# Gated delta rule and a softplus layer on one core: inverses by chunk and by pair, 64x64 tiles, word transposes, longer query runs, a new order

## The chip, the cores and the metric

The kernel runs on one core of a Trainium2 chip. The engines of the core work side by side, each through its own list of instructions in order: TensorE (PE: matmuls, and PEld: its weight loads), VectorE (DVE), ScalarE (ACT), GpSimd (POOL) and SyncE (SP, which here only issues DMAs). The metric is the device time of one execution in microseconds (us). Three runs of the kernel before took 305.52, 309.42 and 303.7 us; the median is 305.52.

## The reference

Four batches of eight heads carry a 48x48 state through 768 steps; the gated readouts of all heads, side by side, go through a layer with softplus.

```python
B, H, S, D = q.shape                      # 4, 8, 768, 48
k_n = k / (np.linalg.norm(k, axis=-1, keepdims=True) + 1e-06)
state = np.zeros((B, H, D, D))
for t in range(S):
    readout = np.einsum('bhd,bhde->bhe', q[:, :, t], state)
    y[:, :, t] = g[:, :, t] * readout
    v_old = np.einsum('bhde,bhd->bhe', state, kt)
    state = state + bt[:, :, :, None] * np.einsum('bhd,bhe->bhde', kt, vt - v_old)
...
x = y.transpose(0, 2, 1, 3).reshape(B * S, H * D)     # 3072 x 384
h = x @ w_in                                          # 384 x 2048
out = (np.maximum(h, 0) + np.log1p(np.exp(-np.abs(h)))) @ w_out
```

## The kernel before

The 768 steps are cut into 12 chunks of 64. Within a chunk the recurrence is solved at once: with the keys' inner products as a strictly lower triangular matrix and beta on the diagonal, the updates of a chunk follow from a 64x64 triangular inverse per batch and head. A partition half (64 rows) holds one pair of batches, so that a tile has 128 partitions and 16 sequences of 48 in its free dimension.

**Front of a chunk** (`front`): keys and queries are loaded from DRAM (`load`, SP's queue; one DMA brings 64 partitions x 16 sequences x 48 numbers as runs of 192 bytes), cast to 16 bits (`cast`), transposed on PE (`trs`, L289), copied out (`kev`), and multiplied with each other (`gram`, L396 and L397; `gramk` and `gramq` for the first two chunks, L326, L327 and L359). The key products go into `kk` (`kkc`), those of keys and queries are masked into `mt` (`mask`, L414).

**Norms** (`norms`): squares on ACT, sums on DVE (`red`, L445), a square root on ACT for the first two pairs, and a power on POOL afterwards (`pow`, L461). The inverse norms go into beta (`lbeta`, from L473) and into the values (`vs`, L657).

**Inverse of a pair of chunks** (`inverse`): one DVE transpose moves the key products so that each partition holds its own 32x32 block (`ln`, L481). Then the two 16x16 diagonal blocks of every 32 are inverted by forward substitution in 15 steps of a product and a sum (`step`, L504 and L511), on DVE for the first pair and on POOL for the other five. A cast (`c16`) and three DVE transposes bring the blocks back (`tn`, L524; `t32`, L534, two). PE extends 16 to 32 (`xmm`, L555; `tmm`, L576 and L582) and prepares the step from 32 to 64 (`zmm`, L608 and L611) on tiles of 32x32.

**Chain of a chunk** (`chain`): `ks` and `qs` (L649) read the state, `w` (L681) subtracts from the values, `umm` (L690 and L694), `u1`, `zu` (L715) and `u2` apply the inverse, `smm` (L735) and `s` give the next state, `ymm` (L765), `y` (L780), `ytr` (L797) and `xt` the gated readout, turned for the layer. Each product comes in two halves of 16 matmuls; umm, zmm and tmm also multiply by an identity to carry a block along.

**Layer** (`dense`): `g1` (L825) multiplies by w_in, `soft` (L837) applies softplus on ACT, `g2` (L852) multiplies by w_out, `o` and `store` bring 128 rows out. Only the chain is serial from chunk to chunk; the layer of earlier chunks fills PE beside it.

Every such step is an item with a number. The long table `_ORDER` at the end of the kernel lists all items in the order in which they are issued, with the letter of the engine (P, D, A, G for POOL, S); `Program.emit` walks through it and hands out buffers from rings as items need them. So the order within every engine is written out by hand, and an engine that waits holds up all items behind it in its own list. The eight loads of the weights (L253) are items on POOL.

Of the kernel before, what the change touches and what calls it, by code (L numbers as in the profile page):

```python
# [10 lines left out]
F32 = mybir.dt.float32  # L11
F16 = mybir.dt.float16
AF = mybir.ActivationFunctionType
# [3 lines left out]
class Ring:  # L17


    def __init__(self, tiles, name):  # L20
        self.tiles = tiles
        self.name = name
        self.free = list(range(len(tiles)))

# [13 lines left out]
class Program:  # L38
# [16 lines left out]
    def emit(self, table):  # L55
        done = set()
        for word in table.split():
            en, no = word[0], int(word[1:])
            it = self.items[no]
            assert en in it.engs and no not in done and all(d.no in done for d in it.deps)  # L60
            for b in it.bufs:
                if b.ap is None:
                    b.slot = b.ring.free.pop(0)
                    b.ap = b.ring.tiles[b.slot]
            it.fn(en)
# [5 lines left out]
        assert len(done) == len(self.items)  # L71


@with_exitstack
def kernel(
# [18 lines left out]
    U = 4 * H  # L94
    DM = H * D
    FF = moe_w_in.shape[1]
    NF = FF // P

# [13 lines left out]
    QUAD = [slice(32 * i, 32 * i + 32) for i in range(4)]  # L112

# [6 lines left out]
    beta_l = pool.tile([P, NC // 2, HC], F32, name="beta_l")  # L120
# [3 lines left out]
    r_k = ring("kf", 4, [P, 2, H, D], F32)  # L124
    r_q = ring("qf", 2, [P, 2, H, D], F32)
    r_v = ring("vf", 4, [P, 2, H, D], F32)
    r_g = ring("gf", 3, [P, 2, H, D], F32)
    r_kn = ring("kn", 5, [P, 2, H, 64], F16)
    r_qn = ring("qn", 2, [P, 2, H, 64], F16)
    r_ksq = ring("ksq", 1, [P, 2, H, D], F32)  # L130
    r_nv = ring("nv", 3, [P, 32], F32)
    r_nl = ring("nl", 2, [P, 32], F32)
    r_bl = ring("bl", 3, [P, 32], F32)
    r_kk = ring("kk", 3, [P, 2, U, HC], F16)
    r_kqt = ring("kqt", 10, [P, 2 * NP * 2 * C + HC], F16)
    r_mt = ring("mt", 10, [P, H, C], F16)
    r_ln = ring("ln", 2, [P, HC, HC], F16)
# [3 lines left out]
    r_t16 = ring("tw", 2, [P, 2, 16, 48], F16)  # L141
    r_tn = ring("tn", 2, [P, U, 16], F16)
    r_xs = ring("xs", 2, [P, U, 16], F16)
    r_td = ring("td", 3, [P, U, HC], F16)
    r_z = ring("z", 4, [P, 16, 2 * HC], F16)
    r_w = ring("w16", 4, [P, H, D], F16)
    r_u = ring("u16", 6, [P, H, D], F16)
    r_s = ring("s16", 6, [P, H, D], F16)
    r_yg = ring("yg", 2, [P, 2, H, D], F16)
    r_xt = ring("xt", 2, [P, 3, 512], F16)  # L150
    r_ga = ring("ga", 18, [P, 512], F16)
# [4 lines left out]

    nc.vector.memset(half_c, 0.5)
    nc.scalar.activation(dummy, half_c[:, :1], AF.Sqrt)
    make_identity(nc, ident32)
    nc.vector.tensor_copy(ident, ident32)  # L160
    for t in r_kn.tiles + r_qn.tiles:
        nc.vector.memset(t[:, :, :, D:], 0.0)
    for r in range(2):
        for hf in range(2):
            l0 = 32 * (2 * r + hf)
            src = beta[2 * r : 2 * r + 2].rearrange(
                "p h (c l r) -> (p h) l c r", l=2, r=64
            )
            for cl in range(2):
                nc.gpsimd.dma_start(  # L170
                    out=beta_l[l0 + 16 * cl : l0 + 16 * cl + 16],
                    in_=src[:, cl, :, 32 * hf : 32 * hf + 32],
                )
# [11 lines left out]
    for t in r_t16.tiles:  # L185
        nc.vector.memset(t, 0.0)
    for t in r_kqt.tiles:
        nc.vector.memset(t[:, 4 * NP * C :], 0.0)
    pat = pool.tile([P, HC], F16, name="pat")
    nc.vector.tensor_tensor(pat, ident[:, :HC], ident[:, 64 : 64 + HC], ALU.add)  # L190
    for t in r_z.tiles:
        nc.vector.tensor_copy(t[:, :, :HC], pat[:, None, :].broadcast_to([P, 16, HC]))
# [19 lines left out]


    tiles, last = {}, {}

    def load(name, x, r, c, b2):
# [5 lines left out]
        def fn(en):  # L222
            ENG[en].dma_start(
                out=b.ap[64 * b2 : 64 * b2 + 64].rearrange("t p h d -> t (p h) d"),
                in_=x[2 * b2 : 2 * b2 + 2, :, t0 : t0 + C].rearrange(
                    "p h t d -> t (p h) d"
                ),
            )

        its.append(  # L230
            add("load", f"{name}{c}.{b2}", "A" if name == "k" and c < 2 and b2 else "S", fn,
                bufs=[b])
        )

    for c in range(NC):
        for name, x, r in (("k", k, r_k), ("q", q, r_q), ("v", v, r_v), ("g", g, r_g)):
# [18 lines left out]


    kn, kn_it, kqt, kqt_it, mt, mt_it = {}, {}, {}, {}, {}, {}

    def kq_of(c, p):
        return kqt[c, p].ap[:, : 4 * NP * C].rearrange("p (n t) -> p n t", n=2 * NP)  # L260

    def front(c, kk):
        cl = c % 2
        parts = 2 if c < 2 else 1
        for p in range(2):
            kqt[c, p] = Buf(r_kqt)
        its, x_of = {}, {}
        for name, ring_ in (("k", r_kn), ("q", r_qn)):
            f, fl = tiles[name, c]
            x = Buf(ring_)  # L270
            x_it = []
            for h in range(parts):
                sl = slice(h, h + 1) if parts == 2 else slice(0, 2)
                x_it.append(
                    add("cast", f"{name}n{c}.{h}", "DGA",
                        lambda en, f=f, x=x, sl=sl: copy(en, x.ap[:, sl, :, :D], f.ap[:, sl]),
                        deps=fl, bufs=[f, x], size=768 // parts)
                )
            x_of[name] = (x, x_it)
            its[name] = []  # L280
            for h in range(parts):
                tp = Buf(p_d)
                ps = [h] if parts == 2 else [0, 1]

                def trs(en, x=x, tp=tp, ps=ps):
                    o = f16ps(tp.ap).rearrange("p (a n t) -> p a n t", a=2, n=NP)
                    for p in ps:
                        for i in range(NP):
                            nc.tensor.transpose(  # L289
                                o[:, p, i],  # L290
                                x.ap[:, p, 2 * i : 2 * i + 2].rearrange("p h d -> p (h d)"),
                                ident,
                            )

                t1 = add("trs", f"{name}{c}.{h}", "P", trs,
                         deps=[x_it[h] if parts == 2 else x_it[0]], bufs=[x, tp],
                         mm=4 * len(ps), mode="full")
                for p in ps:

                    def kev(en, p=p, tp=tp, name=name):  # L300
                        s = f16ps(tp.ap).rearrange("p (a n t) -> p a n t", a=2, t=C)[:, p]
                        kq = kq_of(c, p)
                        copy(en, kq[:, :, :C] if name == "k" else kq[:, :, C:], s)

                    its[name].append(
                        add("kev", f"{name}{c}.{p}", "AD", kev, deps=[t1], bufs=[tp, kqt[c, p]])
                    )
        kn[c], kn_it[c] = x_of["k"]
        mt[c] = [Buf(r_mt), Buf(r_mt)]
        mt_it[c] = []  # L310
        kk_it = []

        def u_of(ap, p, m):
            return ap[:, :, 16 * cl + 8 * p + m : 16 * cl + 8 * p + 8 : 2]

        if c < 2:
            gk = [Buf(p_d), Buf(p_d)]
            for p in range(2):

                def gramk(en, p=p):  # L320
                    for i in range(NP):
                        for r in range(2):
                            for m in range(2):
                                x = kq_of(c, p)[FEAT[m], 2 * i + r, :C]
                                o = gk[m].ap.rearrange("p (n t) -> p n t", n=H)
                                nc.tensor.matmul(o[QUAD[2 * r], NP * p + i], x[:, :HC], x)  # L326
                                nc.tensor.matmul(  # L327
                                    o[QUAD[2 * r + 1], NP * p + i],
                                    x[:, HC:],
                                    x.rearrange("f (x t) -> f x t", x=2)[:, ::-1],  # L330
                                )

                t2 = add("gramk", f"{c}.{p}", "P", gramk, deps=[its["k"][p]],
                         bufs=gk + [kqt[c, p]], mm=32, mode="6432")
                for m in range(2):

                    def kkc2(en, p=p, m=m):
                        copy(
                            en,
                            u_of(kk.ap, p, m).rearrange("p x n t -> p n x t"),  # L340
                            gk[m].ap.rearrange("p (n x t) -> p n x t", n=H, x=2)[
                                :, NP * p : NP * p + NP
                            ],
# [645 lines left out]
```

## Time and profile before

| what | us |
|---|---|
| median of three runs | 305.52 |
| span of the profiled execution | 304.6 |
| PE busy | 241.7 |
| DVE busy | 184.7 |
| ACT busy | 131.4 |
| POOL busy | 120.5 |
| L825 and L852, the layer's matmuls | 82.0 and 77.7 |
| L504 and L511 on POOL, the substitution | 29.0 and 27.7 |
| L837, softplus | 56.3 |

The profile is one execution, seen by the hardware profiler. Its page cuts the span into 40 slices and gives the busy share of each engine in tenths (9 is 90% or more), the clock that TensorE was granted, and the share of the 16 DMA engines. A row of a group reads: line, engine, operation, what it writes and reads, shapes, count | busy time, mean duration in ns | idle time of the engine before it and what ended that. Of the timeline a row reads: start, duration, engine, line, shapes, count [idle before]. In the chain of waits a row is a piece of the path that ended last: start, duration, what. "issue" there is time in which the engine waited for nothing that the profile shows. Waits read: who waited for whom: us in total, times, longest. DMA queues read: packets, megabytes, share of the 16 engines.

### The profile page before, as it was taken

How to read it: one execution, taken by the hardware profiler on the slowest of the kernel's cores; microseconds unless marked ns; L12 is line 12 of the kernel's file. 1: busy time of each engine (PE TensorE's matmuls, PEld its weight loads, DVE VectorE, ACT ScalarE, POOL GpSimd, SP SyncE). 2: the span in 40 equal slices, each digit the busy share in tenths (PEclk: the TensorE clock that was granted, in tenths of full speed). 3: DMA queues.
4: the chain of work that ended last, by engine and by line, in shares of the span. 5: the costliest groups of instructions: out<-in, count | busy, mean ns of one | idle time of the engine just before them, and what ended most of it. 6: DMA issues, size and time to landing. Idle time of an engine off the chain costs nothing.

```text
span 304.6 us, 13469 instructions
## 1 busy us (share of the span) xinstructions
PE 241.7 (79%) x6112; PEld 160.8 (53%) x6112; DVE 184.7 (61%) x348; ACT 131.4 (43%) x250; POOL 120.5 (40%) x219
## 2 busy tenths in 40 slices
PE   1432347789959996869877999969899969999993
PEld 1232236568637763446643565635566635577771
DVE  7789936367696776974873467668486193432100
ACT  4541413347513666244423466613553425433441
POOL 7205335008892588458516203885007810000000
PEclk9999999999969999799985799995999988999999
DMA  9999999999900197983979521341035110002113
GB/s 126 152 140 151 171 143 181 185 168 142 130 2 4 31 163 130 156 132 55 167 109 146 109 56 30 62 68 30 4 83 106 27 28 18 14 22 63 26 26 78
DMA packets 107704, 27.69 MB, mean 91 GB/s; under 512 B 100864, under 2 KB 107648, under 8 KB 107648
## 3 DMA queue, kind: packets, MB, share of 16 engines
q1 hardware_dynamic: 101600, 23.21, 48.5%
q0 software_dynamic: 3968, 3.25, 6.7%
q8 instruction: 47, 0.77, 1.1%
q10 hardware_dynamic: 2080, 0.39, 0.9%
q14 instruction: 9, 0.07, 0.1%
HBM read 25.26 MB, written 4.72 MB: 98 GB/s over the span
## 4 chain that ended last, share of the span: by engine, by line
PE 46%; DVE 21%; POOL 17%; issue 10%; ACT 3%; DMA 2%; DVEq 0%; POOLq 0%; ACTq 0%
PE h L825 14%; PE o L852 14%; POOL tmp L504 8%; POOL tt L511 7%; DVE td L534 4%; DVE tn L524 3%; DVE ln L481 3%; PE d L649 3%; DMA kf<-in_k_dram 2%; PE d L715 2%; DVE tt L511 2%; PE d L289 2%; POOL nn L496 2%; DVE tmp L504 2%; PE d L765 1%
## 5 line engine op out<-in xcount | busy, mean ns | idle before, releaser
L825 PE MATMUL h<-xt,w_in 128*128 128x512 f16 (+1 forms) x384 | 82.0, 352 | 0.0
L852 PE MATMUL o<-w_out,ga 128*128 128x384 f16 x384 | 77.7, 345 | 2.3 <-issue 1.7
L837 ACT ACTIVATE ga<-h 128x512 f16<-128x512 f32 x96 | 56.3, 596 | 40.3 <-PE h L825 33.6
L852 PEld LDWEIGHTS <-ga 128*128 128x128 f16 x384 | 37.3, 102 | 28.9 <-issue 8.9
L825 PEld LDWEIGHTS <-w_in 128*128 128x128 f16 x384 | 36.5, 103 | 22.6 <-issue 5.3
L504 POOL TENSOR_TENSOR tmp<-nn,tt 128x30 f32<-128x30 f32 (+7 forms) x75 | 29.0, 387 | 5.9
L511 POOL TENSOR_TENSOR tt<-tt,tmp 128x30 f32<-128x30 f32 (+7 forms) x75 | 27.7, 369 | 5.9
L534 DVE STREAM_TRANSPOSE td<-tw 128x512 f16<-128x512 f16 x12 | 28.7, 2452 | 0.0
L461 POOL TENSOR_TENSOR nv<-nv,half_c 128x32 f32<-128x32 f32 x4 | 21.8, 5446 | 9.1 <-DVE nv L445 9.1
L200 DVE CAST u<-d 128x384 f16<-128x384 f32 x23 | 12.5, 552 | 19.4 <-PE d L715 15.3
L414 DVE TENSOR_TENSOR mt<-d,mask 128x256 f16<-128x256 f32 x40 | 16.8, 435 | 9.8 <-ACT kk L198 6.7
L198 ACT ACTIVATE u<-d 128x384 f16<-128x384 f32 x25 | 12.1, 492 | 23.4 <-PE d L715 12.7
L198 ACT ACTIVATE kqt<-d 128x512 f16<-128x512 f16 x26 | 15.1, 597 | 16.0 <-PE d L289 10.4
L555 PE MATMUL d<-tn,kk 16*32 16x16 f16 x768 | 7.3, 173 | 16.8 <-DVE tn L524 13.3
L289 PE MATMUL d<-ident,kn 128*128 128x128 f16 x96 | 9.1, 250 | 13.1 <-DVE kn L200 6.1
L198 ACT ACTIVATE osb<-o 128x384 f32<-128x384 f32 x14 | 6.9, 492 | 27.2 <-PE o L852 26.9
L496 POOL TENSOR_TENSOR nn<-ln,bl 128x256 f32<-128x256 f16 x10 | 6.3, 650 | 30.9 <-DVE ln L481 30.9
L649 PE MATMUL d<-s,kqt 48*64 48x48 f16 x704 | 16.7, 192 | 1.7 <-issue 1.4
L649 PEld LDWEIGHTS <-kqt 48*64 48x64 f16 x704 | 13.5, 112 | 8.4 <-issue 7.7
L555 PEld LDWEIGHTS <-kk 16*32 16x32 f16 x768 | 7.1, 93 | 18.8 <-issue 15.2
L657 POOL TENSOR_TENSOR vf<-vf,nv 128x768 f32<-128x768 f32 x8 | 11.8, 1472 | 13.2 <-DMA vf<-in_v_dram 13.2
L780 DVE TENSOR_TENSOR yg<-d,gf 128x384 f16<-128x384 f32 x24 | 12.8, 551 | 5.7 <-PE d L765 5.6
(100 smaller groups left out, 405.1 us busy)
## 6 DMA issues: line engine op xcount, KB each, us to landing
qf<-in_q_dram SPq DMA_DIRECT2D x24, 192.0 KB, 5.7
vf<-in_v_dram SPq DMA_DIRECT2D x24, 192.0 KB, 5.8
gf<-in_g_dram SPq DMA_DIRECT2D x24, 192.0 KB, 5.5
out_dram<-osb SPq DMA_DIRECT2D x48, 96.0 KB, 2.2
kf<-in_k_dram SPq DMA_DIRECT2D x22, 192.0 KB, 5.5
w_in<-in_moe_w_in_dram POOLq DMA_DIRECT2D x4, 384.0 KB, 6.6
w_out<-in_moe_w_out_dram POOLq DMA_DIRECT2D x4, 384.0 KB, 10.2
kf<-in_k_dram ACTq DMA_DIRECT2D x2, 192.0 KB, 4.5
```

The lines of the kernel that those rows point to most:

```text
L198: nc.scalar.activation(o, x, AF.Copy, scale=float(sign))
L289: nc.tensor.transpose(o[:, p, i], x.ap[:, p, 2 * i : 2 * i + 2].rearrange("p h d -> p (h d)"), ident,)
L414: nc.vector.tensor_tensor(mt[c][m].ap[:, NP * p : NP * p + NP], gb[m].ap.rearrange("p (n b) -> p n b", n=NP)[:, :, C:], mask[:, None, :].b ...
L461: lambda en: nc.gpsimd.tensor_tensor(nv.ap, nv.ap, half_c, ALU.pow),
L504: eng.tensor_tensor(t, nn.ap[:, :, j + 1 :, j : j + 1].broadcast_to([P, 2, n, w]), tt.ap[:, :, j : j + 1, :w].broadcast_to([P, 2, n, w]), ...
L511: eng.tensor_tensor(rows, rows, t, ALU.add)
L534: nc.vector.transpose(td.ap.rearrange("p u i -> p i u")[:, 16 * b : 16 * b + 16], tw.ap[:, b, :, c0 : c0 + 32],)
L555: nc.tensor.matmul(uv(xp.ap)[QUAD[qd], u], kk.ap[r, 0, u, :], tn.ap[r, u, :])
L649: nc.tensor.matmul(hd(o.ap)[HALF[r], NP * p + i], kq_of(c, p)[FEAT[m], 2 * i + r, off : off + C], s0[r].ap[FEAT[m], NP * p + i], **start(p ...
L825: nc.tensor.matmul(hp.ap[:, n * b : n * b + n], w_in[:, j, f * P : (f + 1) * P], xt.ap[:, j, t0 : t0 + n], start=(j == 0), stop=(j == 2),)
L837: lambda en, hp=hp, o=gb: nc.scalar.activation(o.ap, hp.ap, AF.Softplus),
L852: nc.tensor.matmul(op.ap[:, :DM], b.ap[:, col + c0 : col + c0 + 128], w_out[:, f, :], start=(f == 0), stop=(f == NF - 1),)
```

## The change

The kernel computes the same. What changes:

- Inversions: the chunks are grouped as [0], [1], [2, 3], ... [10, 11]. Chunk 0 is inverted on DVE, the other six groups on POOL. Chunk 0's work no longer waits for chunk 1's keys in the data; the order decides what runs first.
- The key products, the inverse and the identities beside them lie in 64-wide tiles (`kk`, `td` of 96 columns, `z`, `xs`, with fixed identity columns that are filled once), so that all small products run on 64x64 tiles, 32 matmuls to an item, without separate identity matmuls. In most of them successive matmuls go through all four tiles (`CROSS`).
- The transposes of the inverse move 32-bit words, pairs of 16-bit numbers. For a pair `ln` moves 1024 words, and each of the three transposes out 512; `pick`, and masks in `ca` and `cb`, sort the two chunks of a pair.
- From chunk 1 on, keys are scaled by the inverse norm before the transpose (`kmul`, in place of the cast), so beta and values stay as they are.
- Queries are loaded as runs of 1536 bytes (8 steps x 48 numbers) and put into place by the copy behind the transpose (`qev`).
- Squares, keys, queries, values and gates share one ring of 12 buffers.
- Constants: the first buffer of each ring is set up on DVE, the others by POOL as items (`gset`).
- A new order, with the weights' loads first on POOL.

```diff
+GROUPS = [[0], [1], [2, 3], [4, 5], [6, 7], [8, 9], [10, 11]]
+INV_ENG = "DGGGGGG"
...
+    r_f = ring("f", 12, [P, 2, H, D], F32)
...
+    CROSS = [
+        (r, p, i, m)
+        for i in range(NP)
+        for m in range(2)
+        for p in range(2)
+        for r in range(2)
+    ]
...
+            if name == "q":
+                src = x[:, b2::2, t0 : t0 + C].rearrange(
+                    "b i (g j) d -> b i g (j d)", j=8
+                )
+                ENG[en].dma_start(out=b.ap[:, b2].rearrange("p h d -> p (h d)"), in_=src)
+                return
...
+                def kmul(en, sl=sl, nv=nv):
+                    n = 2 if parts == 1 else 1
+                    ENG[en].tensor_tensor(
+                        kn[c].ap[:, sl, :, :D], kf.ap[:, sl],
+                        nv.ap[:, :NU].rearrange("p (a h) -> p a h", a=2)[:, sl, :, None]
+                        .broadcast_to([P, n, H, D]),
+                        ALU.mult,
+                    )
...
+        def lanes_out(dst, src, blocks, step_):
+            i = words(src.rearrange("p s x j -> p (s x j)")).rearrange(
+                "p (s x w) -> p x w s", s=HC, x=2)
+            o = words(dst.rearrange("p c u t -> p (c u t)"))
+            if pair:
+                o = o.rearrange("p (n k w) -> p k w n", n=32, w=8)[:, blocks::step_]
+                nc.vector.transpose(o, i)
...
+            def xmm(en, cl=cl, xp=xp):
+                for u in range(NU):
+                    for r in range(2):
+                        nc.tensor.matmul(
+                            uv(xp.ap)[HALF[r], u],
+                            kk.ap[HALF[r], cl, u, HC:],
+                            dn.ap[HALF[r], cl, u],
+                        )
...
+        def umm(en):
+            for r, p, i, m in CROSS:
+                nc.tensor.matmul(
+                    hd(up[r].ap)[HALF[r ^ p], 2 * i + m],
+                    td.ap[HALF[r], cl, H * p + 2 * i + m, :C],
+                    w1[m].ap[HALF[r], NP * p + i],
+                )
```

The order's beginning, for POOL, was: casts of keys and queries, the scaling of v0, weights from the ninth item on. It is now: weights w1.3, w1.0, w1.2, w0.2, w0.1, w0.0, the diagonal of chunk 1, w0.3, the first setup, w1.1, the second setup, the scaling of v0, a copy of it, and then chunk 1's inverse. DVE's beginning has chunk 0's keys, the sum of chunk 1's squares, chunk 0's transpose and steps, with the scaling of chunk 1's keys and a mask after the eighth step. PE's list has the X product of chunk 1 behind the second g1 of chunk 0, and that of chunks 4 and 5 right behind the chain of chunk 3.

More of the change, by code (lines that the diff above doesn't have):

```diff
@@ L194 @@
+    setup = [None]
+    for n in range(1, 4):
+        setup.append(add("gset", f"{n}", "G", lambda en, n=n: later(en, n)))
+    for r_ in (r_kn, r_qn, r_tw, r_ta, r_kk, r_td, r_z, r_xs):
+        for n in range(1, len(r_.tiles)):
+            r_.init[n] = setup[n]
     ENG = {"D": nc.vector, "A": nc.scalar, "G": nc.gpsimd, "S": nc.sync}
```

1094 lines of the change are left out of this document (547 added, 547 removed).

## The prediction

> **What bounds the kernel now.** I read the page first: the 40 slices, then the chain that ended last.
>
> ```profile
> PE   1432347789959996869877999969899969999993
> DVE  7789936367696776974873467668486193432100
> PEclk9999999999969999799985799995999988999999
> DMA  9999999999900197983979521341035110002113
> ...
> PE 46%; DVE 21%; POOL 17%; issue 10%; ACT 3%; DMA 2%; DVEq 0%; POOLq 0%; ACTq 0%
> ```
>
> One slice is 7.6 us. TensorE (PE) is nearly idle for seven slices while the DMA is full; afterwards it is busy, with dips that a lower clock digit accompanies. No engine is the bound throughout: PE holds 46% of the chain, inversions (DVE, POOL) most of the rest.
>
> Next the timeline of PE around the second pair's inverse, and the waits.
>
> ```profile
> 86.89 1.19 PE L555 MATMUL d<-tn,kk 16*32 16x16 f16 x128 [3.56 <-DVE tn L524]
> 88.01 5.00 PE L852 MATMUL o<-w_out,ga 128*128 128x384 f16 x16
> ...
> PE d L555 <- DVE tn L524: 13.3, 5, 3.6
> ```
>
> PE waits 3.6 us for the transposed inverse, and then 16 dense matmuls take 5.0 us. The chain of waits gives the full pace, and the pace of small products:
>
> ```profile
> 42.13 1.04 PE d L715 x31
> 43.18 2.28 issue
> 47.66 0.44 PE d L359 x28
> ...
> 171.73 0.50 PE d L715 x30
> 293.09 1.31 PE h L825 x12
> ```
>
> At full pace six 128x256 matmuls take 0.655 us, and four 128x384 ones 0.65, half of the 1.25 at 88 us. So each inversion costs its wait plus some 3 us of half-pace matmuls. The "issue" gaps of 2 us lie where no data was missing; the instruction queue's 47 packets of 16 KB suggest code arriving through full DMA queues.
>
> **PE's own work.** I priced every step in PE's order at its undisturbed duration: 96 g1 x 0.655 + 96 g2 x 0.65 = 125.3 us dense, and small steps of 76.7 (8 transposes 0.45, a gram half 0.35, xmm 0.49, tmm 0.60, zmm 0.52, each sixteen 64x64 products 0.25). Sum 202. PE needs 300.4 - 6.1 = 294.3, so 92 is excess, 42 of it before 60 us. From the X product of chunks 4 and 5 (122.5 us) to the last matmul it needs 143.8 and takes 177.9: excess 34.
>
> **Small products on 64x64 tiles.** Products fall from 6112 matmuls to 4840. Per chunk nine groups of 32 (xmm, tmm, zmm, ks, qs, umm, zu, smm, ymm) and two grams of 16 remain beside transposes. Gramq is the one step of before that rotates over four 64x64 tiles: 28 in 0.44 is 15.7 ns, against 33.5 for the two-tile zu (31 in 1.04) at the same half pace. zu at full pace is 16.7 ns (30 in 0.50), so four tiles come to 7.8, and 32 products to 0.25; I add 0.05 for changes of tile shape. The ends are 0.25 and, if rotation gains nothing, 0.53. xmm and tmm alternate between two tiles: 0.45. Per chunk: transposes 0.9 and 0.34, grams 0.6, xmm and tmm 0.9, seven groups 2.1: 4.8, and 183 in all (179 to 203).
>
> [...]
>
> **The inverse as words.** These rows are by form:
>
> ```profile
> L534 DVE STREAM_TRANSPOSE td<-tw 128x512 f16<-128x512 f16 x12 | 28.7, 2452 | 0.0
> L461 POOL TENSOR_TENSOR nv<-nv,half_c 128x32 f32<-128x32 f32 x4 | 21.8, 5446 | 9.1 <-DVE nv L445 9.1
> L524 DVE STREAM_TRANSPOSE tn<-tw 128x512 f16<-128x512 f16 x6 | 14.3, 2377 | 2.6 <-POOL tw L200 2.4
> L481 DVE STREAM_TRANSPOSE ln<-kk 128x1024 f16<-128x1024 f16 x6 | 11.4, 1907 | 2.2 <-ACT kk L198 2.0
> L473 DVE STREAM_TRANSPOSE nl<-nv 128x32 f32<-128x32 f32 x6 | 1.2, 202 | 0.1
> ```
>
> A pair still has one transpose of 1024 elements in and three of 512 out; only the element doubles. Scattered 2-byte writes cost 4.7 ns each (L534), scattered reads 1.9 (L481). Words appear only in L473, 202 ns for 32, hardly more than other DVE operations of that size. Ends: 1 ns a word (ln 1.0, out 0.6) or per element as now (1.9, 2.4). I take 1.9 and 1.0, nearer to the word row. DVE's other operations, counted in the changed program and priced by their rows, make 155.6 (48 masks x 0.435, 24 u x 0.552, 22 w x 0.556, 8 key products x 0.95, 12 xs x 0.68 the largest), so DVE totals 186 (173 to about 210) against 184.7: the values' scaling and the low transposes go; key scaling, xs and a seventh inversion come.
>
> **POOL.** Six inversions instead of five at 15 us (69.0 to 83.9), nine powers of 16 instead of four of 32: 2.7 each if halved, 5.4 if the cost is fixed; I take 2.7.
>
> **Weights and queries.** All eight weight loads move ahead of everything on POOL, issued from about 4.6 us.
>
> ```profile
> q1 hardware_dynamic: 101600, 23.21, 48.5%
> q0 software_dynamic: 3968, 3.25, 6.7%
> ```
>
> Counting packets in steps of 3 us: from 51 to 60 us queues q0 and q1 move one for one (590 against 596), q1 at 196 a us instead of 780. 3712 weight packets thus hold the input loads back from 6.6 to about 27 us; before, this happened at 31 to 39 and 46 to 61. A query load falls from 1024 packets of 21 ns to 128 of about 100 (the stores' packets of that size): 1.35 to 0.8 us, 13 us of DMA in all, and under the weights it hardly counts. SP's order then gives: k0 at 5.5 as before, k1 10, q0 13.5, v0 29, the second half of g0 39.
>
> **The front, step by step.** DVE has the reduction of k1 ahead of chunk 0's transpose, so that starts at 12.3 (13.8 before) in spite of the smaller chunk; prep and 15 steps take 11.3 as before, plus 3 for chunk 1's scaling, gram pieces and transpose placed between them, plus lockouts:
>
> ```profile
> 24.77 0.80 DVE L504 TENSOR_TENSOR tmp<-nn,tt 128x30 f32<-128x30 f32 x1
> 25.61 1.41 DVE L511 TENSOR_TENSOR tt<-tt,tmp 128x30 f32<-128x30 f32 x1
> ```
>
> These two need 0.21 elsewhere; a POOL cast (24.70, 0.83) and product (25.50, 1.48) run beside them, and each ends with it. POOL's 15 setup operations now fall among the steps: 0 to 6 us, I take 2. X starts about 31 (30.0 before); ymm at 38; y waits for g0 at 39 and DVE's order; the first g1 comes at 43 instead of 52.2.
>
> [...]
>
> POOL's scaling of v0 waits until 29, and chunk 1's inverse is queued behind it: 31 to 46.5. PE has all but two g1 queued behind chunk 1's X product (48), so the early dense work hardly starts before. Three powers, a cast, and chunk 3's gram behind that lead to prep2 at 61.5, the pair's inverse at 76.5, X at 79 (86.9 before); power and inverse again: X of chunks 4 and 5 at **99.5** instead of 122.5. Fixed-cost powers add up to 10.
>
> **Costed at nothing.** ACT comes to 142 by its rows (131.4 before; evictions of 1024 columns at twice 0.6 less a little), half of the span: hidden, except in a chain's own copies, which stay as many. On SP the store of chunk 0's second half stands ahead of the loads of v2 and g2; it waits for the output product at about 58, and v2 is wanted at 81: 20 us of cover; without it chunk 2's chain would wait as long. All loads share 12 buffers instead of 4, 2, 4 and 3; the first that waits for a slow reader is q7, for v0's (31 us), wanted by POOL before 57.
>
> **Sum.** 44.5 of PE's 183 are then done (16 g1, 16 g2, six fronts, four inversions, three and a half chains), 138.5 remain. Later inversions start 10 us or more ahead of their place in PE's order, so most of their waits (3.0 and 3.1 at 202 and 244 us among them) and the half pace behind them go: of 34 excess I keep 20, for code gaps, chain latencies and DVE, which is then busy about 120 of 155 us. The end behind the last matmul stays 4.2 (304.6 - 300.4). 99.5 + 138.5 + 20 + 4.2 = **262**. The profiled span, 304.6, is 0.9 below the median of 305.5, so the forecast stands for both.
>
> **Rivals.**
> - *Transposes cost per element as now.* DVE 210, inverses some 3 us later each: excess 34 and X at 105 give 282 (276 to 296). For it: L534 and L524 agree at 4.7. Chance 0.20.
> - *All waits go.* Excess 8, work 135: 247. Chance 0.08.
> [...]
> - *The tiles do not do what they should*: 0.53 a group, stalls stay: work left 154, X at 106, excess 34: 298 to 302. Chance 0.08.
> - *DVE becomes the bound, slower.* If scattered word writes cost by bytes, 9.3 ns, a transpose out takes 4.7 and ln 3.7: 107 us, DVE 263. In the last 44 us DVE is idle 35 whatever it costs (9.8 busy from 260 us on), and 20 of inner waits at least: 318. It decides from about 4 us per transpose. Against it: L473. Chance 0.12.
>
> The forecast itself, 250 to 276, gets 0.50. A measurement of this kernel separates about 2% from no change. Faster: 0.50 + 0.20 + 0.08 + 0.02 = 0.80; same 0.08; slower 0.12. The range reaches from half of the lighter case to the edge of no change: 243 to 300.
>
> **What would show it.** The word transposes near 1.0 us; a four-tile group of 32 in 0.3; g1 from 43; X of chunks 4 and 5 at 100; later X products without a wait; input loads at about 200 packets a us until 27. It is wrong if DVE's transposes exceed 2.4 us, or if PE's dips return at the inversions.

## The result and the profile after

The changed kernel takes 293.52 us (median of 4 runs, 292.94 to 297.3) against 306.19 for the kernel before on the same chip (4 runs, 303.7 to 309.42): ratio 0.962, interval 0.953 to 0.972. Medians, here and below, are over all runs of a kernel; ratios leave out runs that lie over 1.5% above its fastest. It is faster, as forecast, and inside the range, but by 12.7 us where 43 were forecast. The profiled execution has a span of 292.2.

The page after: five rows of the 40 slices (one is 7.3 us), the two large DMA queues (packets, megabytes, share) and the chain that ended last.

```profile
PE   0303117489995884699997899669997999999993
DVE  7999038467996768897785945268856852230000
POOL 8921688876488989961885058850486000000000
PEclk9999999959999597589999999959999999999998
DMA  7999998970499498547599371211010120121212
...
q1 hardware_dynamic: 82176, 23.60, 47.9%
q0 software_dynamic: 4096, 3.25, 6.9%
...
POOL 39%; PE 31%; DVE 10%; issue 8%; DMA 6%; ACT 4%; POOLq 0%; ACTq 0%; DVEq 0%
```

POOL now holds 39% of the chain (17% before) and is busy for most of the first 125 us, but for 15 to 29 us, where it waits behind the weights (below). PE is still nearly idle for six slices, and dips at 88 to 95 us, at 110 to 124 and at 183 to 197, with the clock at half in or behind each (95.9 to 102.7, 112.9 to 126.5 and 191.4 to 198.2). The longer query runs took 19,400 packets from q1 and hardly any of its time (48.5% before).

This table is read from the timeline of PE: when a step starts, in us. "Layer of 2, 3" is the first g1 of chunks 2 and 3; "rest" is from there to the last matmul.

| kernel | first g1 | X of chunk 3 | layer of 2, 3 | last matmul | rest |
|---|---|---|---|---|---|
| before | 52.2 | 87.4 | 112.0 | 300.4 | 188.4 |
| forecast | 43 | 79 | | 257.8 | |
| changed | 53.9 | 97.5 | 124.3 | 287.9 | 163.6 |

Read across, this is the whole result. Once the layer of chunks 2 and 3 runs, the changed kernel needs 24.8 us less than before (PE is busy for 17.6 us less there, 151.8 instead of 169.3, and idle for 7.2 less, 11.9 instead of 19.1); but that point comes 12.3 us later. The difference is the 12.5 that the last matmul moved.

### The profile page after: what moved, and what is told of

Its sections match the earlier page's. It is cut to its first block, busy times and chain, and to the rows that moved or that the text cites. A ratio compares the mean times of both kernels' runs of the same rounds, so it can differ in the third digit from the quotient of the medians.

```text
span 292.2 us, 11017 instructions
## 1 busy us (share of the span) xinstructions
PE 221.4 (76%) x4840; PEld 146.6 (50%) x4840; DVE 175.3 (60%) x351; ACT 145.8 (50%) x250; POOL 149.8 (51%) x271
## 4 chain that ended last, share of the span: by engine, by line
POOL 39%; PE 31%; DVE 10%; issue 8%; DMA 6%; ACT 4%; POOLq 0%; ACTq 0%; DVEq 0%
POOL tt L605 13%; PE o L923 12%; POOL tmp L598 11%; PE h L896 11%; DMA w_out<-in_moe_w_out_dram 6%; POOL tw L622 4%; POOL nn L588 3%; DVE ln L549 3%; DVE mt L476 2%; POOL nv L351 2%; ACT tw L620 2%; PE d L689 1%; PE d L843 1%; PE d L494 1%; PE d L669 1%
## 5 line engine op out<-in xcount | busy, mean ns | idle before, releaser
L896 PEld LDWEIGHTS <-w_in 128*128 128x128 f16 x384 | 36.2, 100 | 24.8 <-issue 4.1
L605 POOL TENSOR_TENSOR tt<-tt,tmp 128x30 f32<-128x30 f32 (+7 forms) x90 | 36.3, 403 | 7.0
L254 ACT ACTIVATE kqt<-d 128x1024 f16<-128x1024 f16 (+1 forms) x21 | 20.0, 960 | 22.5 <-PE d L400 20.6
L351 POOL TENSOR_TENSOR nv<-nv,half_c 128x16 f32<-128x16 f32 x9 | 26.2, 2914 | 4.6 <-DVE nv L357 2.8
L689 PE MATMUL d<-tb,xs 64*64 64x32 f16 x384 | 9.1, 188 | 12.8 <-DVE xs L678 11.7
L669 PE MATMUL d<-dn,kk 64*64 64x32 f16 x384 | 10.2, 198 | 9.4 <-DVE dn L651 6.0
L494 PE MATMUL d<-kqt 48*64 48x128 f16 (+1 forms) x448 | 11.9, 225 | 5.5 <-ACT kqt L254 3.8
L400 PEld LDWEIGHTS <-kn 128*128 128x128 f16 x96 | 7.7, 116 | 16.1 <-issue 7.6
L689 PEld LDWEIGHTS <-xs 64*64 64x64 f16 x384 | 8.2, 120 | 15.0 <-DVE xs L678 12.5
L254 ACT ACTIVATE kk<-d 128x256 f16<-128x256 f32 x32 | 11.6, 392 | 7.9 <-PE d L494 4.8
L669 PEld LDWEIGHTS <-kk 64*64 64x64 f16 x384 | 9.7, 134 | 11.0 <-issue 7.2
L773 DVE TENSOR_TENSOR w<-f,d 128x384 f16<-128x384 f32 x22 | 11.2, 549 | 4.9 <-PE d L742 3.6
## 6 DMA issues: line engine op xcount, KB each, us to landing
beta_l<-in_beta_dram POOLq DMA_DIRECT2D x8, 10.0 KB, 11.8
```

The source lines that it names most:

```text
L254: nc.scalar.activation(o, x, AF.Copy, scale=float(sign))
L351: lambda en: nc.gpsimd.tensor_tensor(nv.ap[:, :NU], nv.ap[:, :NU], half_c[:, :NU], ALU.pow),
L400: nc.tensor.transpose(o[:, NP * p + i], kn[c].ap[:, p, 2 * i : 2 * i + 2].rearrange("p h d -> p (h d)"), ident,)
L605: eng.tensor_tensor(rows, rows, t, ALU.add)
L669: nc.tensor.matmul(uv(xp.ap)[HALF[r], u], kk.ap[HALF[r], cl, u, HC:], dn.ap[HALF[r], cl, u],)
L689: nc.tensor.matmul(uv(ep.ap)[HALF[r], u], xs.ap[HALF[r], u], tb.ap[HALF[r], cl, u])
```

## The experiments

Times are medians; ratios are against the kernel before, run on the same chip beside each. "Layer", "rest" are those of the table above, read from each kernel's profiled run (e3's took 294.5 us, far above its median, so its steps are left out).

| run | median | ratio, interval | X of 3 | layer | rest |
|---|---|---|---|---|---|
| changed | 293.5 | 0.962 (0.953 to 0.972) | 97.5 | 124.3 | 163.6 |
| e1 beta loads on SP | 290.9 | 0.946 (0.939 to 0.953) | 90.1 | 117.7 | 163.9 |
| e2 one cast on VectorE | 294.0 | 0.956 (0.949 to 0.963) | 92.7 | 119.7 | 167.4 |
| e3 six pair copies on VectorE | 289.4 | 0.944 (0.940 to 0.948) | | | |
| e4 these three | 288.3 | 0.942 (0.938 to 0.946) | 90.1 | 117.1 | 162.1 |
| e5 e4, w_out later | 288.9 | 0.950 (0.940 to 0.960) | 91.9 | 119.4 | 162.4 |
| e6 e4, inverse 1 on VectorE | 283.9 | 0.933 (0.922 to 0.943) | 88.8 | 116.9 | 162.5 |
| e7 two tiles in turn | 298.8 | 0.983 (0.971 to 0.995) | 97.6 | 128.3 | 167.0 |
| e8 transposes twice | 313.4 | 1.030 (1.021 to 1.040) | 99.4 | 128.8 | 178.2 |
| e9 e6, new order | 281.1 | 0.920 (0.911 to 0.928) | 89.5 | 115.3 | 160.7 |
| e10 new order alone | 288.2 | 0.941 (0.934 to 0.948) | 94.3 | 120.1 | 161.6 |
| e11 e6, w_out later | 285.0 | 0.926 (0.915 to 0.938) | 89.4 | 116.6 | 162.1 |
| e12 e6, all weights later | 285.3 | 0.929 (0.920 to 0.937) | 89.9 | 116.8 | 163.1 |
| e13 inverse 1 shortened | 296.8 | 0.976 (0.971 to 0.980) | 92.1 | 121.7 | 168.9 |
| e14 inverse 2, 3 shortened | 293.5 | 0.965 (0.960 to 0.969) | 93.4 | 120.1 | 167.7 |
| e15 inverse 4, 5 shortened | 293.9 | 0.966 (0.956 to 0.977) | 96.4 | 123.8 | 163.9 |

### The front: POOL's queue behind the weights (e1 to e4)

In the changed kernel these groups stand out, by form (count | busy, mean ns | idle time before and what ended it).

```profile
L235 POOL DMA_DIRECT2D beta_l<-in_beta_dram x8 | 4.2, 530 | 14.1 <-DMA w_in<-in_moe_w_in_dram 9.4 <-DMA w_out<-in_moe_w_out_dram 4.7
L651 DVE STREAM_TRANSPOSE tb<-tw 128x256 uint32<-128x256 uint32 x2 | 1.2, 625 | 11.2 <-POOL tw L256 11.2
L256 POOL CAST tw<-tt 128x512 f16<-128x512 f32 x1 | 2.4, 2397 | 0.0
L622 POOL TENSOR_SCALAR tw<-tt,mx 128x512 f16<-128x512 f32 x3 | 10.3, 3417 | 0.2
L620 ACT ACTIVATE tw<-tt,mx 128x512 f16<-128x512 f32 x4 | 10.1, 2516 | 0.8 <-POOL tt L605 0.8
L622 DVE TENSOR_SCALAR tw<-tt,mx 128x512 f16<-128x512 f32 x3 | 4.1, 1366 | 1.9 <-POOL tt L605 1.9
```

The second setup step issues eight small beta loads on POOL, behind the eight weight loads. Seven of the eight issues wait until an earlier weight load has landed, 0.3 to 3.7 us each and 14.1 in all; value scaling, the cast of chunk 0's inverse and the inverse of chunk 1 stand behind them, and VectorE's transpose of that cast waits 11.2. The last three rows are one copy on three engines: 512 columns, each 16-bit number written 64 bytes behind the one before, take 3.4, 2.5 or 1.4 us.

e1 takes the eight loads out of the setup step:

```diff
-                        eng.dma_start(
-                            out=beta_l[l0 : l0 + 16, 2:],
...
+    add("beta", "late", "S", late_beta)
...
-S14 P173
+S14 S1181 P173
```

> The eight late beta loads are issued by SyncE (between its other loads) instead of by GpSimd behind the weight loads; nothing else changes. Theory (the lost time is POOL's queue standing behind the weights at the front): the rest of the setup step ends near 19 us instead of 36, so the cast of chunk 0's inverse (38.7 to 41.0 in the changed kernel) comes at 29 to 32; T product of chunk 0 at 33 to 35 instead of 42.6, first g1 at 45 to 47 instead of 53.9, X product of chunk 1 at 49 to 52 instead of 58.4, and the end 7 to 10 earlier: 284 to 287. Rival A (what was won at the front is given back, because PE or another queue is late later anyway): first g1 as early, but the end 0 to 3 earlier, 290 to 294. Rival B (the input loads under the weights are what holds the front): T product of chunk 0 early, but first g1 still at 52 or later, waiting for the gate rows, and the end unchanged.

e2 and e3 change letters of the order only:

```diff
-D153 D155 G154
+D153 D155 D154
```

> Only the cast of chunk 0's inverse goes from GpSimd to VectorE, behind the one of its first half. Theory: T product of chunk 0 at 32 to 34 instead of 42.6, but umm of chunk 0 still waits for the value scaling on POOL (36.1 to 38.1), so first g1 comes 6 to 7 earlier, at 47; POOL's own work loses only the 2.4 us of the cast, so chunk 1's inverse and all that is queued behind it come 2.4 earlier, and so does the end: 290 to 292. Rival (PE's front is what sets the end, not POOL's queue): the end follows the first g1, 286 to 288.

```diff
-G286 ... G367 ... G529 ... G530 ... G532 ... G611
+D286 ... D367 ... D529 ... D530 ... D532 ... D611
```

> Only the six masked copies of the pairs that POOL makes (three of 512 columns at 3.4 us, three of 256 at 1.4) go to VectorE (1.37 for 512, about 0.4 for 256). Theory: each stands either in front of a transpose or of POOL's next power and inverse, so the X product of chunk 3 comes 2 earlier (95.5 instead of 97.5), POOL's next inverse 3.4 earlier, X of chunk 4 at 116 to 118 instead of 121, X of chunk 9 4 earlier than 191.5; the end 3 to 6 earlier, 287 to 290. Rival (these copies lie beside PE's work): X products a little earlier, the end within 1 us of the changed kernel.

> The three edits of the other runs together. Theory: the gains add up in front of the inverse of chunks 4 and 5, since it is one queue of POOL: its X product at 106 to 110 instead of 121, and the end at 278 to 283. Rival A: PE is then the bound from the first g1 on, and the end comes to 286 to 290 whatever X does.

e1's T product of chunk 0 came at 36.6 (42.6), the first g1 at 49.1, X of chunk 1 at 51.7 (58.4), and the last matmul of the profiled run 6.3 earlier: the way of the theory, but of its figures only X of chunk 1 was met. The median fell only 2.6, to 290.9, into the range of rival A, with runs from 287.5 to 293.9; the clock, below, goes with that spread. e2 brought the first g1 to 45.3, 8.7 earlier, and the layer's start 4.6 earlier, but not the end, at a lower clock (0.881 to 0.926 in its runs). e3 came to 289.4, inside its range; where that gain arises is not shown. e4 gave 288.3, the value of rival A: the gains do not add up.

### What the gains are worth (e7, e8)

e7 turns the loops of the six four-tile groups:

```diff
     CROSS = [
         (r, p, i, m)
+        for p in range(2)
         for i in range(NP)
         for m in range(2)
-        for p in range(2)
         for r in range(2)
     ]
...
```

> The changed kernel, with the loops of the six groups that run over four 64x64 tiles turned so that consecutive matmuls alternate between two tiles only; the same matmuls otherwise. Theory: each group takes 0.45 to 0.5 instead of 0.25, 70 groups in all, 14 to 17 us more of PE's own work; where PE has no slack (behind the X product of chunk 4, 60% of them) it reaches the end: 9 to 12 later than the changed kernel's 293.5, 302 to 306, which would mean that most of what the change gained came from here. Rival (the groups lie in chains that wait for copies anyway): 294 to 297.

e8 issues each `nc.vector.transpose` of the inverses twice:

```diff
                 nc.vector.transpose(o, i)
+                nc.vector.transpose(o, i)
```

> The changed kernel, with every transpose of the inverses (into and out of the lanes) issued twice in a row on VectorE: 31 us more of DVE, about what they would cost at one price per 16-bit element. The prediction's rival said of that price: 20 us more (282 against 262). Theory (only the inverses in front of the X product of chunk 4 are on the path, with some 2 to 3 us each, later ones come ahead of their place): 8 to 12 later than the changed kernel's 293.5, 301 to 306, with X of chunk 3 at 100 to 103 and X of chunk 4 at 127 to 131. Rival (DVE has room everywhere): 294 to 297.

Two rows of PE and two of VectorE from the changed kernel, by form:

```profile
L800 PE MATMUL d<-u,z 64*64 64x48 f16 x384 | 6.2, 198 | 2.1 <-DVE u L256 1.7 <-ACT u L254 0.3
L843 PE MATMUL d<-u,mt 64*64 64x48 f16 x384 | 9.3, 193 | 0.6 <-issue 0.6
...
L549 DVE STREAM_TRANSPOSE ln<-kk 128x1024 uint32<-128x1024 uint32 x5 | 9.7, 1935 | 0.2
L647 DVE STREAM_TRANSPOSE td<-tw 128x512 uint32<-128x512 uint32 x5 | 5.4, 1074 | 2.3 <-POOL tw L622 2.3
```

The same row of zu (L800) in e7:

```profile
L800 PE MATMUL d<-u,z 64*64 64x48 f16 x384 | 8.1, 199 | 1.6 <-DVE u L256 0.7 <-ACT f L334 0.6 <-ACT u L254 0.2
```

32 products start within 0.25 us over four tiles (changed kernel) and within 0.38 to 0.40 over two (e7). So four tiles save 0.13 to 0.15 an item, 9 to 10 us of PE for some 70 items, and 5.3 us of time: less than the theory's 9 to 12, more than the rival allowed. ymm (L843) has as many matmuls as zu and 9.3 us instead of 6.2. Each of its products reads and writes the same partition half, so it has two tiles only, in the changed kernel too, as zu has in e7 (8.1); why it takes longer than that, no run shows.

The doubled transposes add 34 us to VectorE (209.6 busy instead of 175.3) and cost 19.9 us, the price that the prediction's rival had put on transposes at one price per element. Where it arises differs from the expectation: only 4.5 lie ahead of the layer of chunks 2 and 3, and 14.6 in the rest, where VectorE's queue holds the copies of the chains. PE is idle there for 19.7 us instead of 11.9, and its mean clock in that stretch is 0.92 instead of 0.97, so part of the 14.6 is pace and not waiting. Waits of PE in e8 that lie wholly or mostly in the rest:

```profile
PE d L679 <- DVE dn L656: 3.9, 2, 3.6
...
PE d L797 <- DVE z L256: 2.9, 1, 2.9
PE h L906 <- DVE xt L256: 2.8, 2, 2.4
```

### Place of the weights, the series on POOL, the order (e5, e6, e9 to e12)

e5, e11 and e12 move words of POOL's list behind the scaling of v0 (`G633`) and its copy (`G634`); e5 the four w_out loads (`G103` to `G106`), e11 these and the second setup step (`G1`), e12 the w_in loads too:

```diff
-G106 G103 ... G105 G101 ... G100 ... G99 ... G102 ... G104 ... G1 ... G633 ... G634
+G101 ... G100 ... G99 ... G102 ... G633 ... G634 G103 G104 G105 G106 G1
```

> The kernel with the three edits together, and besides the four w_out loads (half of the weight bytes) moved on POOL's queue from the very front to behind the scaling of v0. Theory (under the weights the input loads crawl, so POOL waits for v0 until 31.6 even when its queue is free): v0 and with it the scaling at 22 to 25, chunk 1's inverse from 28.5 (its own transpose) instead of 33.7, X product of chunk 1 at 45 to 47 instead of 51.0, of chunk 3 at 84 to 86 instead of 90.1, and the end 3 to 5 earlier than with the three edits (profiled span 283.4, median 288.3): median 283 to 285. Rival (the same bytes have to come before the gate rows and the keys of chunks 2 and 3 anyway): the scaling earlier, but first g1 not before 46 and X of chunk 3 within 1 us of 90.1, the end unchanged.

> The kernel with the three edits and chunk 1's inverse on VectorE (median 283.9), and only on POOL's queue: the four w_out loads and then the second setup step come behind the scaling of v0 and its copy. In the earlier run with late w_out loads both setup steps ran back to back on POOL from 9.0 to 15.6 and held a VectorE operation of 0.17 us for 6.06 us; here only the first one runs there. Theory (the weights in front hold back v0, the gate rows and the keys): scaling of v0 at 22 to 25 instead of 30.9, umm of chunk 0 at 34 to 36 instead of 37.1, X of chunk 3 at 86 to 88 instead of 88.8, median 281 to 283. Rival (the same bytes then hold back queries, gates and the keys of chunks 2 and 3): scaling early, X of chunk 3 at 89 or later, median 284 to 287.

> As the run beside it, but all eight weight loads behind the scaling of v0 and its copy, w_in first. Theory: without weights in front the scaling comes at 15 to 19, keys of chunks 2 and 3 and the gate rows land 5 or more earlier, umm of chunk 0 at 33 to 35, the first g1 at 45 to 48 (49.9 before), X of chunk 3 at 84 to 87, median 278 to 282. Rival (w_in is then what the first g1 waits for): first g1 at 51 or later, X of chunk 1 and the front behind it in PE's list late with it, median 285 to 290.

The scaling came at 21.4 us in e11 and 14.4 in e12 (30.9 in e6), in e5 the copy behind it at 23.7, and the layer's start did not move by more than 0.3 between e6, e11 and e12: the rivals of e11 and e12 hold. Where the weights stand is neutral in these kernels, where chunk 1's inverse does not queue behind them on POOL. With that inverse on POOL only e5 moved weights, and its front was slower for another reason, seen in VectorE's timeline (first fence) and POOL's (second):

```profile
8.89 6.06 DVE L347 TENSOR_SCALAR nv<-nv 128x16 f32<-128x16 f32 x1 [0.28 <-ACT nv L336]
14.99 0.31 DVE L349 COPY nv<-nv 128x16 f32<-128x16 f32 x1
```

```profile
9.49 1.17 POOL L214 COPY kk<-pat 128x512 f16<-128x512 f16 x2
10.60 1.16 POOL L214 COPY td<-pat 128x512 f16<-128x512 f16 x2
...
12.65 1.16 POOL L214 COPY kk<-pat 128x512 f16<-128x512 f16 x2
13.76 1.16 POOL L214 COPY td<-pat 128x512 f16<-128x512 f16 x2
14.87 0.73 POOL L214 COPY z<-pat 128x256 f16<-128x256 f16 x2
```

An operation that takes 0.17 us in the changed kernel took 6.06 here: it ended at 14.95, when POOL's row of copies had come to its last pair (from 14.87). So one operation lasted nearly as long as a whole row of instructions beside it; what it waited for, the trace does not show.

e6 adds chunk 1's inverse on VectorE, and e9 rearranges e6's lists and 136 engine letters; e10 rearranges the changed kernel's lists alone.

```diff
-INV_ENG = "DGGGGGG"
+INV_ENG = "DDGGGGG"
```

> The kernel with the three edits together, and besides the whole inverse of chunk 1 (30 small steps) on VectorE behind chunk 0's, between the copies of chunk 0's chain, instead of on POOL. Theory (the chain of inverses on POOL, four of them before the X product of chunk 4, sets the first half): POOL is free for the power of chunk 3 at 34 instead of 50.2; the pair inverse of chunks 2 and 3 starts at 60 to 64 instead of 69.8, X of chunk 3 at 80 to 85 instead of 90.1, X of chunk 4 at 104 to 108 instead of 113.8, and the end 6 to 9 earlier than the median of the three edits (288.3): 279 to 283. Rival A (keys of chunks 2 and 3 have to pass DVE and PE first, which the steps now delay): inverse of 2 and 3 not before 68, the end unchanged or later. Rival B (X products come early but PE is bound behind them): X of chunk 4 early, the end only 0 to 3 earlier.

> The kernel with the three edits and chunk 1's inverse on VectorE, with the same items in a new order: the lists of PE, VectorE, ScalarE and GpSimd rearranged, and 136 copies, casts, scalings and masked copies given to another engine that can do them; loads, weights, PE's matmuls and transposes unchanged. Theory (what is left of the forecast was lost in queues, by items that were ready and stood behind others that waited; from the X product of chunk 4 on PE has 139 us of own work and takes 166 in this kernel without the new order, 27 of excess, and 30 more between the first g1 and there): the excess falls by 12 to 18, in the second half above all; the layer's work of chunk 2 starts 5 to 8 earlier than 129, the X products of chunks 8 and 10 7 to 15 earlier than 192.3 and 215.3, and the median comes to 266 to 273, against 283.9 without the new order. Rival A (the inverses set the pace, not the queues): X of chunk 3 still at 88 to 92, PE waits there as before, the median 280 to 285. Rival B (contention of VectorE and GpSimd, which is then higher, eats it): single operations on VectorE several times their length, the median above 285.

> The changed kernel with only the order of its items rearranged: every item stays on its engine, chunk 1's inverse on POOL, the late beta loads inside the second setup (which now comes behind chunk 0's cast on POOL's queue). Theory: as in the run beside it; the front gains some 3 to 6 by the setup step alone (T product of chunk 0 at 36 to 39 instead of 42.6), the rest comes from the queues: the layer's work of chunk 2 from 126 to 130 instead of 136.2, X of chunk 8 at 186 to 190 instead of 203.6, the median 270 to 278 instead of 293.5. Rival A (engine assignments and the price of the copies on POOL, not the order, are what costs): 287 to 292. Rival B (the order is worth the 7 of the front that the first run showed, no more): 284 to 288.

e6's median is 4.4 below e4's, less than its theory's 6 to 9: POOL was free early, but the pair's inverse still started at 68.4, since chunk 3's keys passed VectorE and PE late (its rival A for the place). In the profiled runs the last matmul even comes at 279.4 against e4's 279.2, so the timeline does not show the 4.4; e4's runs had clocks of 0.907 to 0.946, e6's of 0.934 to 0.951. e9 is the fastest of all, 281.1, and beats both kernels; but it missed its 266 to 273 and came out as its rival A had it (X of chunk 3 at 89.5, 280 to 285). Its page, whose chain reaches back over its last part only:

```profile
PE   0321254989995866889999899999999999999993
...
PEclk9999999999999865686999999999999999999999
...
PE 45%; ACT 2%; DVE 1%; issue 0%; DVEq 0%; ACTq 0%
```

From 133 us to the last slice PE never falls below eight tenths, and the clock is full. Of its rest of 160.7 PE is idle for 3.9 us only, against 11.9 in the changed kernel; so, some half pace before 133 us apart, that rest is PE's own pace through this list, and less waiting can hardly lower it further. e10 stopped at 288.2, where its rival A had it: the order alone, the setup's new place in it included, gains 5.3.

### Which serial stage sets the start of the layer (e13 to e15)

Each leaves out the last seven of fifteen substitution steps of one inverse (so that inverse is incomplete):

```diff
         def step(en, j):
+            if gi == 2 and j >= 8:
+                return
             n, w = 15 - j, j + 1
```

> The changed kernel without the last seven of the fifteen substitution steps of chunk 1's inverse on POOL (6.2 us less there, so the inverse of chunk 1 is not complete). Theory (a series on POOL: setup, inverse of 1, powers, inverse of 2 and 3): X of chunk 1 at 52 instead of 58.4, the pair's inverse (77.0) and X of chunk 3 (97.5) 4 to 6 earlier, the layer's work of chunks 2 and 3 at 118 to 120 instead of 124.3, the median 287 to 289. Rival (the keys of chunk 3, through VectorE's and PE's queue, hold the pair's inverse, not POOL): the pair's inverse at most 2 earlier, the median 291 to 294.

> The changed kernel without the last seven substitution steps of the inverse of chunks 2 and 3 (6.2 us less on POOL, the inverse not complete). Theory (it is on the path to the layer's work in full): X of chunk 3 at 91 to 92 instead of 97.5, the layer's work of chunks 2 and 3 at 118 to 119, the median 287 to 288. Rival (PE still works off the layer of chunk 1 in front of that X product): X at 95 or later, the median 291 to 294.

> The changed kernel without the last seven substitution steps of the inverse of chunks 4 and 5 (some 5 us less on POOL, the inverse not complete). Theory (its masked copies wait for POOL at 116.6 on VectorE and ScalarE, with the copies of chunk 3's chain queued behind them, so it delays the layer of chunks 2 and 3, which does not need it): chain of chunk 3 ends 3 to 4 earlier, the layer's work at 120 to 121 instead of 124.3, the median 289 to 291. Rival (only chunk 3's own chain sets it): 123.5 to 124.3, the median 292.5 to 294.

All three theories fail by the median, and e13 is slower than the changed kernel although it does less. By the timeline e13 and e14 do move the layer's start, by 2.6 and 4.2 (e15 by 0.5, as its rival had it), but the rest grows by 5.3 and 4.1. Busy time by stretch in the changed kernel, with PE's clock third from the right:

```profile
220.00:225.00 5.00, 3.92 (x56) 2.20 (x55) 2.56 (x3) 3.92 (x6) 3.73 (x8) 1.00 0.02 3
225.00:230.00 5.00, 3.92 (x169) 2.89 (x169) 4.61 (x7) 2.58 (x5) 0.00 (x0) 1.00 0.18 41
```

The same in e14:

```profile
220.00:225.00 5.00, 2.80 (x109) 1.95 (x107) 4.34 (x6) 3.99 (x5) 1.31 (x1) 0.92 0.00 0
225.00:230.00 5.00, 5.00 (x105) 3.03 (x104) 2.73 (x5) 0.56 (x2) 0.00 (x0) 0.50 0.19 43
```

And the wait in between, in the changed kernel's timeline of PE and in e14's:

```profile
226.07 0.34 PE L923 MATMUL o<-w_out,ga 128*128 128x384 f16 x1 [2.16 <-ACT ga L908]
```

```profile
223.04 0.34 PE L925 MATMUL o<-w_out,ga 128*128 128x384 f16 x1 [2.20 <-ACT ga L910]
```

The same wait for softplus, 2.2 us long, is followed by the full clock in one kernel and by half of it in the other, from 224.2 to 231.0, where four of g2's matmuls take 1.46 us instead of 0.82 until 231. What decides between the two outcomes, no run shows. Between 50 us and the last matmul, windows of 0.2 us show nine stretches of half clock in the traces before and after: two of 3.4 us, two of 6.8 and one of 13.7 before, three of 6.8 and one of 13.7 in the changed kernel.

In e1's four runs the time is longer where the mean clock is lower (clock, time):

```
0.944 287.54    0.935 290.11    0.923 291.69    0.909 293.88
```

6.3 us lie between equal programs. e13's two runs of 296.7 had 0.904 and 0.907 (a third, of 333.8, had 0.696). e14's three runs (293.88, 293.54 and 292.64) had 0.920 to 0.924; the changed kernel's one run at 0.919 took 297.3, its other three, at 0.938, took 293. So the 4.2 won at the layer's start seem to be there and lost to the lower clock; with one run to compare, this is likely and not shown.

## Why the prediction was right in sign and wrong in size

**PE's own work: right in the count, short in the prices.** By the prediction's prices the work behind the X product of chunk 4 is 138.6 (forecast 138.5); the small products took longer than priced, as the third point shows.

**Word transposes: right**, 1.07 and 1.94 us (1.0 and 1.9 forecast), and POOL's power of 16, 2.91 (2.7). That their price matters, 20 us by e8, was the size given to the rival.

**Four tiles: right in mechanism, too small in the terms.** 0.25 us for 32 was measured, but "seven groups 2.1" counted ymm among them (0.60 to the next item), and four others took 0.37 with the change of shape, not 0.30: 2.7 a chunk; X and T products took 1.2 instead of 0.9. That is 0.9 a chunk, by estimate some 7 us for the eight chunks or so behind the X product of chunk 4. The bound of 0.53 for two tiles was too high (0.38 to 0.40 in e7), and the rival's other half, 'stalls stay', was nearer: without rotation the kernel takes 298.8, inside its 298 to 302, but by another sum.

**The front: the first step that failed.** "POOL's 15 setup operations now fall among the steps: 0 to 6 us, I take 2" left out that this item also issues eight DMAs on a queue full of weights: 14.1 us of waiting and 4.2 of issue. The first g1 came at 53.9 instead of 43, X of chunk 1 at 58.4 instead of 48. e1 takes back 4.8 of the one and 6.7 of the other. That the weights hold v0 back is right (its scaling came at 30.9 us in e6 and at 14.4 in e12), but the start of the layer did not move with it.

**The copies behind an inverse: a term that is too small.** "Costed at nothing" speaks of a chain's own copies, "which stay as many"; for those of the inverse the sum allows no more than the 2.5 us between its end and X of chunk 3 (76.5 to 79), and 5.0 were measured (92.5 to 97.5). Before, one cast stood behind a pair's inverse, in runs of 16 numbers (its median on VectorE 0.46 us; the mean below holds one of 1.68). Now four masked copies stand there, two of them of 512 columns with a step of 64 bytes, at 1.4 to 3.4 us each. The step is what differs most; no run changes it alone. The row before:

```profile
L200 DVE CAST tw<-tt 128x512 f16<-128x512 f32 x5 | 4.0, 799 | 7.8 <-POOL tt L511 7.8
```

The chain of waits after the pair's inverse in the changed kernel:

```profile
92.50 3.36 POOL tw L622
95.86 2.57 POOL nv L351
98.43 1.17 POOL nn L588 x2
...
112.39 2.88 POOL nv L351
...
116.56 0.46 ACT tw L620
118.60 0.69 ACT ta L620
119.29 0.38 ACT u L254
```

A copy and a power stand before the next inverse, another power inside it, and ACT's copies of that inverse in front of chunk 3's u.

**X of chunk 4** came at 121.0 instead of 99.5, and these 21.5 us are most of the error. 10.4 of them are there by X of chunk 1 (the front). 5.1 more come up to the pair's inverse (77.0 instead of 61.5; POOL is idle for 4.3 right before it, waiting for the transposed keys), 3.0 in and behind that inverse up to X of chunk 3 (97.5 instead of 79), and 3.0 up to X of chunk 4. At X of chunk 4, e1 takes back 6.6, and e6, which moves the setup's loads, the copies and one inverse, 7.4; e9, whose list puts that product elsewhere, starts the layer 9.0 earlier. The other 12 to 14 no run removes, and their cause stays open. Whether chunks 0 and 1 as a pair, as before, would, was not tried.

**Later waits: the second step that failed.** "Most of their waits and the half pace behind them go: of 34 excess I keep 20" kept 28.3. PE is idle for 11.8 of the 166.9 us behind that product (16.1 of 177.9 before), at a mean clock of 0.96 (0.92 before): waits and half pace fell, but did not go. The largest waits left:

```profile
PE d L669 <- DVE dn L647: 3.4, 1, 3.4
PE o L923 <- ACT ga L908: 2.2, 1, 2.2
PE h L896 <- DVE xt L256: 2.0, 1, 2.0
```

At 191.5 an X product has waited 3.4 for a transpose behind POOL's masked copies, and half the clock follows, to 198.2; at 226 softplus is late behind ACT's masked copy of 2.5 us. That dips returning at the inversions would break the forecast was named in its last paragraph. But waits alone are not the 8.3: e9 has 8.0 us less of them from the layer on, and its rest is only 2.9 shorter (160.7). By size the small products priced too low, some 7 us, are the larger part; this is worked out from rows, and no run shows it by itself.

**Sum.** 21.5 late at X of chunk 4, 8.3 more excess, 0.1 in the count, 0.1 at the end, from 262: 292, the span measured. That the time fell into the range is luck: the range held since it reached to the rivals, whose causes did not occur. Of the rivals themselves, VectorE as the bound is refuted (175.3 us busy), though e8 shows how little further it is. The 0.02 in the sum of the chances is that of a floor under the time between starts of matmuls, which no run shows: over four tiles they start 8 ns apart (0.25 us for 32).

## What to carry to other kernels

A moved item carries everything that it issues: look for its DMAs and ask what they queue behind. Look for a point from which the rest of a kernel takes nearly the same time in most variants (here the layer of chunks 2 and 3: 161 to 164 us in ten of the fifteen changed kernels in the table whose steps were read), and price what moves that point or that rest. When a change gives data a new layout, price the copies that write it, not only the operations that read it. A gain of a few us in front is not settled by medians alone where the clock varies: compare the timeline and runs of equal clock.

## What the runs showed of the hardware

- Masked copies of 128x512 that write 16 bits at every 64th byte: 3.42 us on POOL, 2.52 on ACT, 1.37 on VectorE (changed kernel, L622 and L620); before, a plain cast of 128x512 in runs of 16 numbers: 0.61 on POOL, 0.46 on VectorE (L200).
- A transpose of 32-bit words took 1.94 us for 1024 and 1.07 for 512 (changed kernel, L549 and L647), 1.9 to 2.1 ns a word, as much as a 16-bit read with a stride before (1.91 for 1024, L481).
- 32 products on 64x64 tiles start 8 ns apart over four tiles (changed kernel), 12 to 13 over two (e7). ymm, whose products read and write the same partition half, took 9.3 us for 384 against 6.2 of zu (changed kernel, L843 and L800).
- A VectorE operation took 6.06 us beside a row of POOL copies (e5, L347), and 0.17 in the changed kernel.
- A 2.2 us wait of PE was followed by half the clock for 6.8 us in one program (e14) and by the full clock in another (the changed kernel).
